# RWKV attention and a max-of-three feed-forward on one core: the order of 1593 pieces by one rank each instead of due times by kind and stage

## The chip, the cores and the metric

The kernel runs on 1 core of one Trainium2 chip. The metric is the device time of that core in microseconds (us); a smaller number is better. Five engines work beside each other, each through its own queue in order: TensorE (PE in the profile), VectorE (DVE), ScalarE (ACT), GpSimd (POOL), and SyncE (SP), which here only issues DMAs.

## What is computed

An attention with a decaying state, token by token, and a feed-forward network behind it. Shapes: batch 4, 8 heads, 768 tokens, head size 48; the feed-forward takes 3072 rows of 384 values through 768 hidden units.

```
for t in range(S):
    kt, vt, rt = (k[:, :, t], v[:, :, t], r[:, :, t])
    cur = np.einsum('bhd,bhe->bhde', u[None] * kt, vt)
    y[:, :, t] = np.einsum('bhd,bhde->bhe', rt, state + cur)
    state = w[None, :, :, None] * state + np.einsum('bhd,bhe->bhde', kt, vt)
...
h = np.maximum(np.maximum(x @ w1, x @ w2), x @ w3)
return (h @ w_out).astype(np.float32)
```

## The kernel before

**Tiling.** The 768 tokens are cut into 12 chunks of 64. A chunk's attention is done in two halves, q = 0 and q = 1, of 4 heads each. Per half PE makes the scores (`sc`), the values (`va`: scores times v, plus r times the state) and the update of the state (`ke`). A chunk's feed-forward is 18 groups `up` (6 blocks f of hidden units times 3 weight matrices i, each of 9 matmuls of 128x256, line 693) and the groups `dn` (three blocks of outputs, 18 matmuls each, mostly cut in two: 15 for f = 0 to 4 and 3 for f = 5). fp32 values are split into two fp16 numbers, a high and a low part; the high parts are made by ACT, the low parts by DVE (`kdl`, `ktdl`, `vdl`, `sdl`, `rl`, `al`: lines 449, 451, 490, 601) or POOL (`hl`, line 721). I write up c.f.i, dn c.m and sc, va, ke c.q, with the chunk first.

**Stages.** Chunks 0 and 1 take the attention's matmuls in fp32, chunks 2 and 3 in fp16 parts on 64-row corners of the array, and from chunk 4 on as 128-row matmuls of spread blocks, which SP copies with DMAs (`kb`, `ktb`, `vb`, `sb`, lines 436 and 437). In chunks 0 to 2 DVE scales k and r and makes the products; from chunk 3 on POOL does (lines 480, 499, 500, 516, 522). In the first 60 us the fp64 weights of the feed-forward are loaded as 8 "words" and made into fp16 parts (ACT lines 351 and 358, DVE lines 355 and 361); word 7 belongs to the second half of `dn`. 22 pieces `stir` of three matmuls each on zeros fill PE at the start.

**What an `up` holds.** Its result lies in one of four PSUM banks (`psm`). For i = 0 ACT copies it to a tile `m` (line 708), for i = 1 and 2 DVE takes the maximum into `m` (line 712), and only then is the bank free for the fourth next group. Then ACT makes `hh` of `m` (line 715) and POOL `hl`. `dn` takes a bank of the same four. `feat`, the tile of k and r by features, has two buffers; the load for the next chunk waits until the old one's last reader, the low part `rl`, is done.

**What sets the order.** The work is written as 1593 calls of `do`. Each gives an engine, a cost, what is read and written, which buffers are taken, and a due time of its own (`due`, in units of chunks). `Plan.order` is a list scheduler: of the pieces that can start earliest by its own clock, it takes the one with the smallest `due` and puts it behind the others on its engine. The result is the program's order on each engine, which the chip then follows. Before, a table `SHIFT` with one row for each kind of piece and one column for each of five stages was added to the due time. Costs are in `ISSUE`, `dma`, `helping` and the calls of `do`; `near` stands for DVE's low parts beside POOL.

**The end.** A check of the inputs' ranges ends in a flag (`count`, `flag`); every engine reads it once, ahead of the first piece in the program's order that touches dn 11.2 (line 1157), and a general path, not taken here, follows behind the program.

Of the kernel before, what the change touches and what calls it, by code (L numbers as in the profile page):

```python
# [7 lines left out]
F32 = mybir.dt.float32  # L8
# [10 lines left out]
P = 128  # L19
# [11 lines left out]
FEATURE = 2  # L31
HELPED = dict(scale=3, product=3, diagonal=3, decay=3)
# [41 lines left out]
class Plan:  # L74
# [6 lines left out]
    SHIFT = {  # L81
        "sp feat": (0.06, 2.41, 0.07, -2.37, 0),
        "sp tok": (4.64, -12.96, -5.22, 0.22, 0),
        "pe blank": (-0.35, 0, 0, 0, 0),
        "pool pad": (0, -0.41, -0.49, 0, 0),
        "dve kT": (0.95, 1.8, 0, 0, 0),
        "dve rT": (-2.97, 3.27, 0.98, 0, 0),
        "act ru": (-3.24, 2.09, 0, 0, 0),
        "pe bo": (-20.47, 6.44, 0, 0, 0),
        "dve am": (1.11, 102.24, -0.18, -0.19, 0.43),  # L90
        "pe sc": (-3.66, -0.77, -0.03, -0.83, -0.79),
        "pool vz": (-5.54, 0, 0, 0, 0),
        "act apart": (0.53, 0, 0, 0, 0),
        "pe va": (-1.26, 17.06, -22.44, -45.09, 3.03),
        "act xh": (-2.11, 6.29, 19.78, -2.05, -0.03),
        "dve xl": (-0.63, -5.4, -2.29, -1.83, 0.76),
        "act xsq": (0, -4.27, 17.76, -6.93, -1.42),
        "act u": (0, 1.78, 0, 0, 0),
        "dve tkf": (0, -7.35, 0, 0, 0),
        "pe turned": (0, -0.4, 0, 0, 0),  # L100
        "act tkt": (0, -2, 0, 0, 0),
        "pe stir": (0, 0.62, 1.56, 0.64, 1.31),
        "sp word": (3.62, 3.5, 0, 0, 0),
        "act ztop": (-5.52, -0.56, 0, 0, 0),
        "dve word": (2.04, 0, 0, 0, 0),
        "act his": (0.41, -4.8, 0, 0, 0),
        "dve lo": (1.13, -2.95, 0, 0, 0),
        "pe kp": (0.04, -16.13, 0, 0, 0),
        "act kt": (-0.4, -0.46, 0, 0, 0),
        "pe ke": (-10.27, -1.26, 0.08, 0, 0),  # L110
        "act state": (0, -0.83, 0, 0, 0),
        "act sq": (0, 0, -3.6, 6.45, -0.3),
        "act sd": (0, 14.27, 0, 0, 0),
        "dve state": (-1.48, -1.03, 1, -1.84, 0),
        "act sdh": (0, -0.64, 23.47, -0.59, 0),
        "dve sdl": (-4.22, 1.55, 7.23, -1.96, 0),
        "sp x3": (0, 2.95, -1.73, -0.89, 0.43),
        "pe up": (0, -3.62, 0.01, -0.2, -0.43),
        "act m": (-0.7, -4.9, 0, 1.38, -1.96),
        "dve m": (93.3, -556.17, 6.75, 0.9, 1.16),  # L120
        "act hh": (-2.49, -6.05, 2.12, -0.02, -11.37),
        "pool hl": (2.58, 5.89, 0.11, -4.17, 3.89),
        "dve hl": (0, -1.12, 1.62, 0, -0.03),
        "pe dn": (0, -1.32, -44.06, -0.15, 0.87),
        "act io": (0, -1.2, 1.65, -2.57, 0),
        "sp io": (0, -0.82, -6.31, -0.75, 2.37),
        "act kdh": (0, -1.05, -4.12, 0.03, 0.27),
        "dve kdl": (0, -5.77, 1.73, 1.56, 0),
        "act rh": (0, -2.11, 0, 2.07, 3.23),
        "dve rl": (0, 6.31, 0.65, 0.14, -1.72),  # L130
        "dve a": (0, -5.82, 10.67, 18.29, 0.93),
        "act am": (0, 0, 0.68, 0, 0),
        "act ah": (0, -2.27, 0, 24.09, -0.46),
        "dve al": (0, 1.56, -1.03, -0.22, -0.05),
        "dve kdec": (0, 3.63, -1, 0, 0),
        "act ktdh": (0, 8.15, -0.28, -1.81, 0),
        "dve ktdl": (0, -0.05, -0.41, -1.02, 0),
        "act vdh": (0, -0.74, 0, 2.92, -4.09),
        "dve vdl": (0, -1.06, 1.77, 0, 0.91),
        "pool kT": (0, 0, -8.52, 20.12, 0),  # L140
        "pool rT": (0, 0, -0.62, 12.91, -3.47),
        "pool am": (0, 0, 0, 0, 0.93),
        "pool kdec": (0, 0, -1.31, -0.98, 0),
        "sp sb": (0, 0, 0, 0.83, 0),
        "sp kb": (0, 0, 0, 33.45, 5.43),
        "sp ktb": (0, 0, 0, 0.5, 0),
        "sp vb": (0, 0, 0, 10.43, 3.71),
        "act wsq": (0, 0, 0, 1.63, 1.62),
        "sp again": (0, 0, 0, 0, 6.95),
        "dve ends": (0, 0, 0, 0, 3),  # L150
        "dve good": (0, 0, 0, 0, -2.56),
        "pe count": (0, 0, 0, 0, 1.34),
        "dve flag": (0, 0, 0, 0, 0.09),
    }
# [4 lines left out]
    def do(self, due, eng, cost, fn, reads=(), writes=(), takes=(), move=0, near=0, parts=1, counts=1.0, corner=False):  # L159


        n = len(self.todo)
        new = [t for _, t in takes]
        made = (*new, *writes, *reads)[0]
        kind = eng + " " + (made if isinstance(made, str) else made[0])
        stage = sum(due >= x for x in self.CLASSES)
        base = due
        due += self.SHIFT.get(kind, (0,) * 5)[stage]
        need = {self.wrote[k] for k in (*reads, *writes) if k in self.wrote}
        for k in writes:  # L170
# [85 lines left out]
def kernel(ctx, tc, feat, tok, wu, ut, ws, wo, cst, out):  # L256
# [29 lines left out]
    def load_tok(c, q):  # L286
        t = raw.tile([P, 3, 2, B, D], F32, name="tok")
        nc.sync.dma_start(out=t, in_=tok[c, q])
        raws.setdefault((c, q), {}).update(k=t[:, 0], r=t[:, 1], v=t[:, 2])
        return t  # L290

    def load_v(c, q):
        t = raw.tile([P, 2, B, D], F32, name="v1", bufs=4)
        nc.sync.dma_start(out=t, in_=tok[c, q][:, 2])
        raws.setdefault((c, q), {}).update(v=t)
# [307 lines left out]
    def keys(c, q):  # L603
        t = raws[c, q]
        t["ke"] = bank(D)
        if c < WHOLE:
            whole(t["ke"], D, (t.pop("kt") if c < FEATURE else units(t["k"]), units(t["v"])))
        else:
            split(c, t["ke"], [ktd[q]], [ktb], D, [lambda b, i: vd[q].dense[:, b, i, 0:D]])
# [261 lines left out]
    plan = Plan(dict(feat=2, tok=3, raw64=3, v1=4, ru=1, kt=1, psa=2, psv=2, psm=4, rh=2, rl=2, am=2, a=2, ah=2, al=2, x=2, m=3, io=3, hh=1, hl=1))  # L871
# [4 lines left out]
    def dma(due, fn, move, reads=(), writes=(), takes=(), eng="sp", n=1):  # L876
        do(due, eng, n * Plan.ISSUE[eng], fn, reads, writes, takes, move, 0, n)

    def helping(c, columns, what):
        return ("pool", 0.05 + 2.5e-3 * columns) if c >= HELPED[what] else ("dve", dve(columns))  # L880

# [147 lines left out]
    def leave_x(c, q, due):  # L1029
# [34 lines left out]
    def ffn(c):  # L1064
        x = [("xh", c), ("xl", c), ("x3", c)]
        for f in range(NF):
# [24 lines left out]
            do(due - 0.1, *(("dve", dve(TOK)) if lows_by(c, f) is nc.vector else ("pool", 0.7)), lo, reads=[m, ("hh", c, f), *([("hl", c)] if f else [])],  # L1091
# [76 lines left out]
def _layout(inputs):  # L1168
# [29 lines left out]
    tk = np.stack([tokm(inputs["k"]), tokm(inputs["r"]), tokm(inputs["v"])], axis=3)  # L1198
# [26 lines left out]
```

## Time and profile before

| | us |
|---|---|
| median of 3 runs | 382.52 (381.89 to 382.58) |
| the profiled execution | 382.55 |
| its span, first to last instruction | 380.8 |
| PE busy within the span | 373.0 |
| DVE, ACT, POOL busy | 250.3, 243.1, 188.8 |

The span is what the trace covers; 1.75 us of the execution lie outside it. A row of the trace has a start in us from the span's begin, then the time, engine, line and tiles, and in brackets the idle time of the engine ahead of it with what ended it. Matmuls overlap, so a group's own length is a little longer than its share of PE; the distance from one group's start to the next is what it costs.

### The profile page before, as it was taken

How to read it: one execution, taken by the hardware profiler on the slowest of the kernel's cores; microseconds unless marked ns; L12 is line 12 of the kernel's file. 1: busy time of each engine (PE TensorE's matmuls, PEld its weight loads, DVE VectorE, ACT ScalarE, POOL GpSimd, SP SyncE). 2: the span in 40 equal slices, each digit the busy share in tenths (PEclk: the TensorE clock that was granted, in tenths of full speed). 3: DMA queues.
4: the chain of work that ended last, by engine and by line, in shares of the span. 5: the costliest groups of instructions: out<-in, count | busy, mean ns of one | idle time of the engine just before them, and what ended most of it. 6: DMA issues, size and time to landing. Idle time of an engine off the chain costs nothing.

```text
span 380.8 us, 13578 instructions
## 1 busy us (share of the span) xinstructions
PE 373.0 (98%) x5660; PEld 335.8 (88%) x5660; DVE 250.3 (66%) x457; ACT 243.1 (64%) x623; POOL 188.8 (50%) x190
## 2 busy tenths in 40 slices
PE   8999999989999999999999999999999999999995
PEld 6888988878898999999899999999999999989885
DVE  5599999899968647558567667767567565123250
ACT  2899859788566647656556655755655935993621
POOL 8500333899995576466546647537836411020120
PEclk9999999999999999999999999999999999999999
DMA  8885836162995987969995996996996883740301
GB/s 293 324 305 188 339 123 216 72 241 59 286 271 129 257 243 198 273 157 289 271 262 144 268 274 173 265 262 185 247 246 190 213 205 89 245 137 17 99 2 49
DMA packets 28420, 77.12 MB, mean 203 GB/s; under 512 B 4865, under 2 KB 12993, under 8 KB 27329
## 3 DMA queue, kind: packets, MB, share of 16 engines
q1 hardware_dynamic: 28064, 75.96, 68.9%
q8 instruction: 46, 0.75, 0.8%
q10 hardware_dynamic: 288, 0.23, 0.2%
q14 instruction: 22, 0.17, 0.2%
HBM read 38.38 MB, written 4.72 MB: 113 GB/s over the span
## 4 chain that ended last, share of the span: by engine, by line
PE 84%; DVE 7%; issue 2%; DMA 2%; POOL 2%; ACT 1%; SPq 0%; POOLq 0%; DVEq 0%
PE psm L693 63%; PE psv L538 8%; PE psa L538 3%; PE psm L689 3%; PE psa L548 2%; PE psv L548 1%; DMA tok<-in_tok_dram 1%; PE psv L541 1%; DMA feat<-in_feat_dram 1%; PE psa L582 1%; DVE m L712 1%; POOL feat L480 1%; DVE kd L449 1%; DVE sd L451 1%; DVE vd L451 1%
## 5 line engine op out<-in xcount | busy, mean ns | idle before, releaser
L693 PEld LDWEIGHTS <-w 128*128 128x128 f16 x2592 | 249.2, 98 | 30.6 <-issue 1.8
L693 PE MATMUL psm<-x,w 128*128 128x256 f16 x1944 | 225.2, 273 | 1.0 <-DVE m L712 1.0
L721 POOL TENSOR_TENSOR hl<-m,hh 128x256 f16<-128x256 f32 x60 | 47.1, 786 | 125.0 <-ACT hh L715 125.0
L712 DVE SCALAR_TENSOR_TENSOR m<-psm,m 128x256 f32<-128x256 f32 x144 | 60.4, 419 | 59.5 <-PE psm L693 48.8
L715 ACT CAST hh<-m 128x256 f16<-128x256 f32 x72 | 28.9, 401 | 52.8 <-DVE m L712 52.5
L480 POOL TENSOR_TENSOR feat<-feat,wrt 128x512 f32<-128x512 f32 x36 | 51.2, 1440 | 20.5 <-DVE m L712 10.5
L693 PE MATMUL psm<-hh,w 128*128 128x256 f16 x432 | 55.8, 273 | 0.0
L463 ACT ACTIVATE junk<-tok 128x384 bf16<-128x384 f32 x72 | 37.3, 518 | 3.0 <-DMA tok<-in_tok_dram 2.0
L708 ACT ACTIVATE m<-psm 128x256 f32<-128x256 f32 x72 | 27.2, 378 | 16.8 <-PE psm L693 15.9
L693 PE MATMUL psm<-hl,w 128*128 128x256 f16 x216 | 33.4, 273 | 0.5 <-DVE hl L721 0.5
L499 POOL TENSOR_TENSOR am<-tok,u_sb 128x384 f32<-128x384 f32 x18 | 20.2, 1125 | 24.5 <-DVE al L601 20.4
L490 DVE TENSOR_TENSOR rl<-feat,rh 128x512 f16<-128x512 f32 x20 | 17.6, 880 | 11.4 <-ACT rh L485 11.4
L670 DVE SCALAR_TENSOR_TENSOR x<-psv,x 112x512 f16<-112x512 f32 (+2 forms) x24 | 16.1, 673 | 12.6 <-ACT x L667 12.6
L516 POOL TENSOR_TENSOR am<-cs,a 128x512 f32<-128x512 f32 x18 | 20.6, 1145 | 6.3 <-DVE a L507 6.1
L538 PE MATMUL psv<-rh,sb 128*128 128x64 f16 x256 | 23.6, 193 | 0.0
L538 PE MATMUL psv<-ah,vb 128*128 128x64 f16 x256 | 23.6, 193 | 0.0
L538 PE MATMUL psv<-al,vb 128*128 128x64 f16 x128 | 22.7, 193 | 0.0
L538 PE MATMUL psv<-rl,sb 128*128 128x64 f16 x128 | 22.7, 193 | 0.0
L538 PEld LDWEIGHTS <-vb 128*128 128x128 f16 x384 | 21.1, 98 | 0.4
L500 POOL TENSOR_TENSOR am<-am,tok 128x384 f32<-128x384 f32 x18 | 20.7, 1148 | 1.4
L738 ACT ACTIVATE io<-psm 128x256 f32<-128x256 f32 x36 | 13.0, 380 | 12.3 <-PE psm L693 12.0
L507 DVE TENSOR_REDUCE a<-am 128x8 f32<-128x384 f32 x20 | 11.0, 549 | 14.2 <-POOL am L500 14.2
(124 smaller groups left out, 580.1 us busy)
## 6 DMA issues: line engine op xcount, KB each, us to landing
tok<-in_tok_dram SPq DMA_DIRECT2D x26, 576.0 KB, 6.2
feat<-in_feat_dram SPq DMA_DIRECT2D x24, 512.0 KB, 4.8
raw<-in_ws_dram SPq DMA_DIRECT2D x6, 1152.0 KB, 7.7
kb<-kd SPq DMA_DIRECT2D x16, 256.0 KB, 5.6
vb<-vd SPq DMA_DIRECT2D x16, 256.0 KB, 5.9
sb<-sd SPq DMA_DIRECT2D x16, 256.0 KB, 5.5
out_dram<-io SPq DMA_DIRECT2D x31, 128.0 KB, 5.4
kb<-kd SPq DMA_DIRECT2D x16, 248.0 KB, 5.9
```

The source lines that it names most:

```text
L463: nc.scalar.activation(out=junk[:, 0:U * D].rearrange("p (u d) -> p u d", u=U), in_=src, func=AF.Square, scale=scale, accum_out=stat[:, ki ...
L480: helper(c, "scale").tensor_tensor(out=t[n], in0=t[n], in1=tb, op=ALU.mult)
L490: nc.vector.tensor_tensor(out=t["rl"], in0=units(t["rT"]), in1=t["rh"], op=ALU.subtract)
L499: helper(c, "product").tensor_tensor(out=w.rearrange("p (g b) d -> p g b d", g=2), in0=t["r"], in1=by_token(u_sb, q), op=ALU.mult)
L500: helper(c, "product").tensor_tensor(out=w, in0=w, in1=units(t["k"]), op=ALU.mult)
L516: helper(c, "diagonal").tensor_tensor(out=t["a"], in0=eye.unsqueeze(1).broadcast_to([P, U, C]), in1=t.pop("sum").unsqueeze(2).broadcast_to ...
L538: nc.tensor.matmul(out=ps[:, i, :], lhsT=block[k].on[a][i], rhs=prods[k](b, i), **flags)
L693: nc.tensor.matmul(out=ps, lhsT=a, rhs=b, start=first and n == 0, stop=last and n == len(prods) - 1)
L708: nc.scalar.mul(out=m, in_=ps, mul=by)
L712: nc.vector.scalar_tensor_tensor(out=m, in0=ps, scalar=by, in1=m, op0=ALU.mult, op1=ALU.max)
L715: nc.scalar.copy(out=h[0][:, f, :], in_=m)
L721: lows_by(c, f).tensor_tensor(out=h[1][:, f, :], in0=m, in1=h[0][:, f, :], op=ALU.subtract)
```

## The change

`SHIFT` goes, and with it the due times as an order. In its place stands `RANK`, a table with one number for each of the 1593 pieces, 0 to 1592, in the order in which they are written; `due` is set to it. The scheduler is otherwise the same: the rank decides only between pieces that can start at the same time by its clock, so a piece does not stand exactly where its rank says.

Several costs that the scheduler's clock uses are changed too: a DMA's issue is 0.58 for the spread copies and 0.74 for the copies inside x (0.45 before), POOL's work for the attention is 12% longer before chunk 6, and POOL's `hl` 0.82 before chunk 5 (0.7 before). No instruction's work changes by that. The three kinds of token tile stand as r, k, v in memory and not as k, r, v; sizes and numbers of loads stay. A new `FLIPPED` equals `FEATURE`, so that the new `load_kv` is never called.

```diff
+FLIPPED = 2
...
-    SHIFT = {
-        "sp feat": (0.06, 2.41, 0.07, -2.37, 0),
...
+    RANK = (
+        6, 51, 69, 17, 70, 33, 370, 317, 349, 309, 302, 280, 378, 412, 413, 410, 518, 331, 447, 700, 24, 39, 20, 13,
...
-        due += self.SHIFT.get(kind, (0,) * 5)[stage]
+        due = self.RANK[n]
...
-        raws.setdefault((c, q), {}).update(k=t[:, 0], r=t[:, 1], v=t[:, 2])
+        raws.setdefault((c, q), {}).update(r=t[:, 0], k=t[:, 1], v=t[:, 2])
...
-    def dma(due, fn, move, reads=(), writes=(), takes=(), eng="sp", n=1):
-        do(due, eng, n * Plan.ISSUE[eng], fn, reads, writes, takes, move, 0, n)
+    def dma(due, fn, move, reads=(), writes=(), takes=(), eng="sp", n=1, each=0.45):
+        do(due, eng, n * each, fn, reads, writes, takes, move, 0, n)
...
-        return ("pool", 0.05 + 2.5e-3 * columns) if c >= HELPED[what] else ("dve", dve(columns))
+        return ("pool", (1.12 if c < 6 else 1.0) * (0.05 + 2.5e-3 * columns)) if c >= HELPED[what] else ("dve", dve(columns))
...
-            dma(due, lambda: spread(nc.sync, dst, src), 2.4, reads=[*keys, *(("pad", n) for n in range(14))], writes=[name], n=2)
+            dma(due, lambda: spread(nc.sync, dst, src), 2.4, reads=[*keys, *(("pad", n) for n in range(14))], writes=[name], n=2, each=0.58)
...
-            do(due - 0.1, *(("dve", dve(TOK)) if lows_by(c, f) is nc.vector else ("pool", 0.7)), lo, reads=[m, ("hh", c, f), *([("hl", c)] if f else [])],
+            do(due - 0.1, *(("dve", dve(TOK)) if lows_by(c, f) is nc.vector else ("pool", 0.82 if c < 5 else 0.7)), lo, reads=[m, ("hh", c, f), *([("hl", c)] if f else [])],
...
-    tk = np.stack([tokm(inputs["k"]), tokm(inputs["r"]), tokm(inputs["v"])], axis=3)
+    tk = np.stack([tokm(inputs["r"]), tokm(inputs["k"]), tokm(inputs["v"])], axis=3)
```

In the rows below, lines of the change stand one lower than those of before (L360 for L361, and so on).

**DVE, around the end of the weights' conversion.** `w7` is the low part of word 7 (line 361), `raw64` its upper step (line 355), `feat` a scaling of k or r of chunk 2 in place (line 480), `rl` the low part of r that frees a `feat` buffer, `m` the maxima of the feed-forward. Before:

```order
L355 SCALAR_TENSOR_TENSOR raw64_773<-raw64_773,ztop1_113 128x1152
L712 SCALAR_TENSOR_TENSOR m_923<-psm_899,m_923 128x256
L480 TENSOR_TENSOR feat_795<-feat_795,wrt_127 128x512
L712 SCALAR_TENSOR_TENSOR m_923<-psm_911,m_923 128x256
L480 TENSOR_TENSOR feat_795<-feat_795,wrt_127 128x512
L361 SCALAR_TENSOR_TENSOR w7_110<-raw64_773,w7_110 128x1152
L449 TENSOR_TENSOR kd0_140<-feat_795,kd0_140 128x8x64
L712 SCALAR_TENSOR_TENSOR m_972<-psm_978,m_972 128x256
L670 SCALAR_TENSOR_TENSOR x_802<-psv1_159,x_802 112x512
L712 SCALAR_TENSOR_TENSOR m_972<-psm_996,m_972 128x256
L451 SCALAR_TENSOR_TENSOR vd0_144<-tok_800,vd0_144 128x8x48
L490 TENSOR_TENSOR rl_1035<-feat_795,rh_991 128x512
```

Of the change:

```order
L489 TENSOR_TENSOR rl_968<-feat_793,rh_954 128x512
L711 SCALAR_TENSOR_TENSOR m_703<-psm_926,m_703 128x256
L711 SCALAR_TENSOR_TENSOR m_937<-psm_956,m_937 128x256
L498 TENSOR_TENSOR am_1032<-tok_808,u_sb_101 128x384
L499 TENSOR_TENSOR am_1032<-am_1032,tok_808 128x384
L354 SCALAR_TENSOR_TENSOR raw64_789<-raw64_789,ztop1_113 128x1152
L711 SCALAR_TENSOR_TENSOR m_1051<-psm_1039,m_1051 128x256
L506 TENSOR_REDUCE a_1067<-am_1032 128x8
L479 TENSOR_TENSOR feat_871<-feat_871,wrt_127 128x512
L711 SCALAR_TENSOR_TENSOR m_1051<-psm_1053,m_1051 128x256
L360 SCALAR_TENSOR_TENSOR w7_110<-raw64_789,w7_110 128x1152
L479 TENSOR_TENSOR feat_871<-feat_871,wrt_127 128x512
```

`rl` of chunk 2, behind `w7` before, now stands ahead of it, and chunk 2's products and the scaling of its second half have come in between.

**ACT, the same place.** `psm_1070` is the result of up 1.1.0, `kd1` the high part of chunk 2's scaled k, which reads the last row above. Before, `kd1` and the first `m` of chunk 1:

```order
L738 ACTIVATE io_1089<-psm_1037 128x256
L485 CAST rh_1091<-feat_989 128x512
L514 ACTIVATE am_1054<-cs_99,a_1087 128x64 x8
L444 ACTIVATE kd1_141<-feat_989 128x8x64
L738 ACTIVATE io_1173<-psm_1068 128x256
L444 ACTIVATE ktd1_143<-tok_993 128x8x48
L708 ACTIVATE m_1191<-psm_1161 128x256
```

Of the change:

```order
L513 ACTIVATE am_1032<-cs_99,a_1067 128x64 x8
L707 ACTIVATE m_1113<-psm_1091 128x256
L714 CAST hh_761<-m_1051 128x256
L443 ACTIVATE kd1_141<-feat_871 128x8x64
L707 ACTIVATE m_1136<-psm_1070 128x256
```

On PE three groups of chunk 1 (up 1.1.0, 1.0.0, 1.0.1) now run ahead of dn 0.1 and dn 0.0, which came first; dn 0.0 takes the bank that `m_1136<-psm_1070` frees, and that copy stands behind `kd1`.

**DVE, in chunk 2's feed-forward.** `psm_2577` is up 2.4.1, `psm_2472` up 2.1.2 (before: `psm_2586` and `psm_2411`). Before:

```order
L712 SCALAR_TENSOR_TENSOR m_2375<-psm_2411,m_2375 128x256
L601 TENSOR_TENSOR al_2439<-am_2020,ah_2425 128x512
L449 TENSOR_TENSOR kd0_140<-feat_2256,kd0_140 128x8x64
L712 SCALAR_TENSOR_TENSOR m_2455<-psm_2441,m_2455 128x256
L712 SCALAR_TENSOR_TENSOR m_2455<-psm_2460,m_2455 128x256
L507 TENSOR_REDUCE a_2485<-am_2457 128x8
L490 TENSOR_TENSOR rl_2565<-feat_2256,rh_2552 128x512
L712 SCALAR_TENSOR_TENSOR m_2539<-psm_2541,m_2539 128x256
L712 SCALAR_TENSOR_TENSOR m_2539<-psm_2555,m_2539 128x256
L712 SCALAR_TENSOR_TENSOR m_2604<-psm_2586,m_2604 128x256
```

Of the change:

```order
L711 SCALAR_TENSOR_TENSOR m_2400<-psm_2472,m_2400 128x256
L450 SCALAR_TENSOR_TENSOR sd1_147<-state_154,sd1_147 128x8x48
L448 TENSOR_TENSOR kd0_140<-feat_2207,kd0_140 128x8x64
L448 TENSOR_TENSOR ktd0_142<-tok_1541,ktd0_142 128x8x48
L489 TENSOR_TENSOR rl_2589<-feat_2207,rh_2572 128x512
L448 TENSOR_TENSOR ktd1_143<-tok_1729,ktd1_143 128x8x48
L711 SCALAR_TENSOR_TENSOR m_2587<-psm_2577,m_2587 128x256
```

Five low parts, of five tiles, now stand between two maxima where three stood among four other maxima.

More of the change, by code (lines that the diff above doesn't have):

```diff
@@ L80 @@
     CLASSES = (0.0, 1.0, 2.0, 10.0)
-    SHIFT = {
-        "sp feat": (0.06, 2.41, 0.07, -2.37, 0),
[L83 to L154, printed above, removed]
@@ L156, in __init__ @@
+    RANK = (
[67 rows of a table added]
+    )
     def __init__(self, bufs):
@@ L288, in load_tok, with load_kv @@
         nc.sync.dma_start(out=t, in_=tok[c, q])
-        raws.setdefault((c, q), {}).update(k=t[:, 0], r=t[:, 1], v=t[:, 2])
+        raws.setdefault((c, q), {}).update(r=t[:, 0], k=t[:, 1], v=t[:, 2])
         return t
+    def load_kv(c, q):
+        t = raw.tile([P, 3, 2, B, D], F32, name="tok")
+        nc.sync.dma_start(out=t[:, 1:], in_=tok[c, q][:, 1:])
+        raws.setdefault((c, q), {}).update(k=t[:, 1], v=t[:, 2])
     def load_v(c, q):
-        t = raw.tile([P, 2, B, D], F32, name="v1", bufs=4)
+        t = raw.tile([P, 2, B, D], F32, name="v1", bufs=2 * FLIPPED)
         nc.sync.dma_start(out=t, in_=tok[c, q][:, 2])
@@ L606, in keys @@
         if c < WHOLE:
-            whole(t["ke"], D, (t.pop("kt") if c < FEATURE else units(t["k"]), units(t["v"])))
+            whole(t["ke"], D, (t.pop("kt") if c < FLIPPED else units(t["k"]), units(t["v"])))
         else:
@@ L868, in general @@
                     put(m, leaving(ps, P, 1.0))
-    plan = Plan(dict(feat=2, tok=3, raw64=3, v1=4, ru=1, kt=1, psa=2, psv=2, psm=4, rh=2, rl=2, am=2, a=2, ah=2, al=2, x=2, m=3, io=3, hh=1, hl=1))
+    plan = Plan(dict(feat=2, tok=3, raw64=3, v1=2 * FLIPPED, ru=1, kt=1, psa=2, psv=2, psm=4, rh=2, rl=2, am=2, a=2, ah=2, al=2, x=2, m=3, io=3, hh=1, hl=1))
     do = plan.do
@@ L904, in fetched @@
         dma(due, lambda: load_feat(c, q), 1.8, reads=behind, writes=["fetched"], takes=[("feat", ("feat", c, q))])
+        if c < FLIPPED:
+            dma(due, lambda: load_v(c, q), 0.85, reads=behind, writes=["fetched"], takes=[("v1", ("tok", c, q))])
+            return
         if c < FEATURE:
-            dma(due, lambda: load_v(c, q), 0.85, reads=behind, writes=["fetched"], takes=[("v1", ("tok", c, q))])
+            dma(due, lambda: load_kv(c, q), 1.67, reads=behind, writes=["fetched"], takes=[("tok", ("tok", c, q))])
             return
@@ L912, in late_squares @@
         dma(due, lambda: do_tile(t, load_tok(c, q)), 2.5, reads=[("begun", int(due))], writes=["fetched"], takes=[("tok", t)])
-        for kind, n in enumerate((1, 0, 2)):
+        for kind, n in enumerate(range(3)):
             do(due + 0.2, "act", 0.62, lambda kind=kind, n=n: square_sum(units(T[t][:, n]), kind, c, q), reads=[t], writes=[("sq", c, q, "rkv"[kind])])
@@ L959, in before_keys @@
         t = ("tok", c, q)
-        if c < FEATURE:
+        if c < FLIPPED:
             do(due - 0.30, "pe", 0.94, lambda: flipped(c, q), reads=[("feat", c, q), ("kT", c, q)], takes=[("psa", ("kp", c, q))], counts=0.5, corner=True)
@@ L1042, in leave_x @@
             if c:
-                dma(due + 0.06, lambda: x_last(T["x", c]), 0.4, reads=[hi, lo], writes=[rest], n=2 * NJ)
+                dma(due + 0.06, lambda: x_last(T["x", c]), 0.4, reads=[hi, lo], writes=[rest], n=2 * NJ, each=0.74)
             do(due + 0.9, "act", 0.97, lambda: x_sum(c, T["x", c]), reads=[hi, rest], writes=[("xsq", c)])
```

66 rows, old and new, of the table RANK are left out of this document.

## The prediction

> **What bounds the kernel now.** First the page's busy times, then a table of windows: for each stretch its length, then the busy time of PE, of PE's weight loads, DVE, ACT and POOL (with instructions in brackets), the granted clock, and the DMA engines' share and rate. Last, what PE waited for.
>
> ```profile
> span 380.8 us, 13578 instructions
> ...
> PE 373.0 (98%) x5660; PEld 335.8 (88%) x5660; DVE 250.3 (66%) x457; ACT 243.1 (64%) x623; POOL 188.8 (50%) x190
> ...
> 0.00:25.00 25.00, 23.36 (x459) 19.61 (x460) 15.83 (x30) 16.02 (x31) 13.47 (x24) 1.00 0.85 310
> 25.00:60.00 35.00, 35.00 (x617) 31.35 (x615) 34.23 (x52) 28.04 (x53) 7.09 (x5) 1.00 0.58 208
> 60.00:100.00 40.00, 38.19 (x926) 33.49 (x921) 37.04 (x58) 31.67 (x91) 33.80 (x28) 1.00 0.53 173
> 100.00:160.00 60.00, 60.00 (x842) 54.62 (x840) 40.10 (x75) 36.48 (x100) 41.39 (x39) 1.00 0.86 231
> 160.00:260.00 100.00, 99.54 (x1411) 91.00 (x1409) 67.64 (x119) 58.74 (x154) 58.04 (x58) 1.00 0.87 237
> 260.00:376.90 116.90, 116.86 (x1427) 105.69 (x1425) 55.46 (x127) 71.79 (x198) 35.01 (x38) 1.00 0.56 149
> 376.90:380.80 3.90, 0.00 (x0) 0.00 (x0) 0.00 (x0) 0.38 (x1) 0.00 (x0) 1.00 0.16 50
> ...
> PE psv L682 <- DVE still L277: 1.1, 1, 1.1
> PE psm L693 <- DVE m L712: 1.0, 1, 1.0
> PE psv L541 <- DVE x L670: 0.7, 1, 0.7
> PE psa L548 <- issue: 0.6, 1, 0.6
> PE psm L693 <- DVE hl L721: 0.5, 1, 0.5
> ```
>
> PE is the bound from 1.1 to 376.9 us, and the change gives it the same matmuls. So the new time is the old one, less the waits that go, plus the waits and turns that come. Of PE's 7.8 idle us, 1.1 lie ahead of its first matmul and 3.9 behind its last (copy out and landing, which the new order has as well). What an order can win is the rest: 0.58 in the first 25 us, 1.81 between 60 and 100, 0.46 at dn 4, **2.85 us in all, 0.7%**. The clock is 1.00 in every stretch, so nothing is to be had there. The other reading of the table matters as much: from 25 to 100 us DVE is busy 71.3 of 75 us. In that stretch there are two full engines, and a new order on DVE is paid there.
>
> **Waits that go.** The 1.81 us of chunks 1 to 3 are PE waiting for DVE's `x` and `m`. Since DVE is nearly full there, they go only if PE comes later or DVE's low parts come quicker. The first happens (below), so I take 1.3 of the 1.81 away and leave 0.5, the bounds being 0 and 1.81. The 0.46 at dn 4.0 is the wait for the last `hl`; between the last `up` of chunk 4 and its use the new order has one more group, up 5.0.0 (0.98 us), so all of it goes. The 0.58 at 14 us waits for nothing that the trace shows; I leave it, with 0 and 1.2 as ends. Together **-1.8**.
>
> **Turns.** Each passage of PE between 64-row corners and the whole array costs:
>
> ```profile
> 17.06 0.72 PE psv L548 x32
> ...
> 25.07 0.98 PE psm L693 x9
> 26.05 0.85 PE psv L548 x32
> ...
> 28.77 1.09 PE psm L693 x9
> ```
>
> In this chain of waits the same `ke` takes 0.72 behind another corner group and 0.85 behind an `up`; an `up` takes 0.98 behind whole-array work and 1.09 behind corners. That is 0.12 a turn. PE's order has 38 turns before and 42 now, all before 120 us: **+0.5**.
>
> **First new wait: dn 0.0.** First, DVE and POOL hold each other up:
>
> ```profile
> 49.20 0.41 DVE L712 SCALAR_TENSOR_TENSOR m<-psm,m 128x256 f32<-128x256 f32 x1
> 49.53 0.83 DVE L480 TENSOR_TENSOR feat<-feat,wrt 128x512 f32<-128x512 f32 x1
> 50.61 0.68 DVE L480 TENSOR_TENSOR feat<-feat,wrt 128x512 f32<-128x512 f32 x1
> 51.21 1.35 DVE L361 SCALAR_TENSOR_TENSOR w<-raw,w 128x1152 f16<-128x1152 f32 x1
> 52.48 1.16 DVE L449 TENSOR_TENSOR kd<-feat,kd 128x512 f16<-128x512 f32 x1
> ...
> 57.88 0.55 DVE L507 TENSOR_REDUCE a<-am 128x8 f32<-128x384 f32 x1
> ...
> 51.23 1.86 POOL L721 TENSOR_TENSOR hl<-m,hh 128x256 f16<-128x256 f32 x1 [1.42 <-ACT hh L715]
> 63.61 2.71 POOL L480 TENSOR_TENSOR feat<-feat,wrt 128x512 f32<-128x512 f32 x2 [10.53 <-DVE m L712]
> ...
> 367.08 0.67 POOL L721 TENSOR_TENSOR hl<-m,hh 128x256 f16<-128x256 f32 x1 [3.53 <-ACT hh L715]
> ```
>
> `hl` takes 0.67 alone and 1.86 when `w7` (line 361) has begun just before it; the `kd` behind that waits for `hl` and takes 1.16 in place of 0.68; a scaling begun while `hl` runs takes 0.83 in place of 0.68. Whoever is second waits for nearly the rest of the first. The rows do not show a weight step (line 355 or 361) that finds POOL at work already. [...]
>
> Now the race, from the end of up 0.5.1, with these rows and:
>
> ```profile
> 50.48 0.38 ACT L708 ACTIVATE m<-psm 128x256 f32<-128x256 f32 x1
> ...
> 51.04 0.64 ACT L444 ACTIVATE kd<-feat 128x512 f16<-128x512 f32 x1
> 51.57 0.62 ACT L485 CAST rh<-feat 128x512 f16<-128x512 f32 x1
> ...
> 53.25 1.26 PE L693 MATMUL psm<-hh,w 128*128 128x256 f16 x10
> ...
> 54.89 1.25 PE L693 MATMUL psm<-hh,w 128*128 128x256 f16 x10
> ...
> 59.19 4.26 DMA feat<-in_feat_dram
> ```
>
> PE has up 0.5.2, three groups of chunk 1 and dn 0.1 ahead of dn 0.0: 4 x 0.98 + 1.64 (53.25 to 54.89) = 5.56 us. Then it needs the bank of up 1.1.0. That bank waits for ACT, ACT's copy for `kd1`, and `kd1` for DVE's row of six: maximum 0.33 (49.20 to 49.53), sum 0.47, scaling 0.60, maximum 0.33, `w7` 1.27 (51.21 to 52.48), scaling 0.69, together 3.69; ACT 0.53 for `kd1` (51.04 to 51.57) and 0.38; about 0.25 for the three hand-overs: 4.85. Undisturbed, PE has 0.7 to spare.
>
> But POOL comes in. `rl`, which frees the `feat` buffer for chunk 3, now stands ahead of the last two weight steps. The load takes 4.26 us; DVE's work from there to `w7` is about 4.7 (three maxima, two products of 0.5, a weight step of 1.3, sum, scaling, maximum). So POOL's two scalings of chunk 3 (2.71, some 1.27 each undisturbed) start about 0.4 ahead of `w7`. Before, they ran at 63.6, past all this. `w7` is held 0.75 and the scaling behind it 1.1. That makes 6.7 against 5.56: a wait of 1.15. If DVE is also late by 0.5, as a queue that is 98% full tends to be, 1.65; if the load lands a microsecond later, `w7` comes first, 0.75 goes, and 0.4 remains; if nothing collides, 0. I take **+1.2**.
>
> **Second new wait: up 2.5.0**, which needs the bank that `m_2587<-psm_2577` frees. Chain and timeline:
>
> ```profile
> 74.69 0.80 DVE rl L490
> 75.49 1.27 DVE vd L451
> 76.76 1.27 DVE sd L451
> ...
> 78.37 0.94 DVE ktd L449
> ...
> 107.93 1.40 PE psv L538 x48
> ```
>
> From the end of up 2.1.2 PE has six `up` and one `va` to do: 6 x 0.98 + 1.40 = 7.28. DVE has a maximum, five low parts, a maximum. Alone the five would take 2.6 (0.68 for two of 512, 0.55 for three of 384, less 0.08 of overlap each). In the rows above, with POOL at work, four take 4.28, which makes 5.35 for five, and 6.35 at the 1.27 of the longest. With the maxima and hand-overs that is 3.6, 6.3 or 7.3 against 7.28, and a low part stands ahead of the first maximum as well, up to 0.9 more. So 0 to 0.9. POOL is busy 85% and 69% in the two stretches around, so the disturbed rows are the nearer: **+0.5**.
>
> **Sum.** 382.55 (the profiled execution, 0.03 over the median of 382.52) - 1.8 + 0.5 + 1.2 + 0.5 = 382.95, **383.0**: a gain on old waits that is spent on turns and two new ones.
>
> **Rivals.**
> - *Slower: DVE and POOL collide everywhere.* Both new waits at their full price, 1.65 and 0.9, and the 1.81 of chunks 1 to 3 stays: 382.55 - 0.46 + 0.5 + 1.65 + 0.9 = 385.1. It decides by whether POOL's scaling of chunk 3 begins ahead of `w7` and DVE is then late by half a microsecond. For it speaks DVE's 71.3 of 75 us; against it, that each new wait makes PE late and gives DVE time for the next one. 0.18.
> - *Faster: no collision forms.* All 2.27 go, only the turns come: 380.8, and 380.2 if the 0.58 goes as well. Chunk 3's `feat` would have to land over 2 us later than I reckon; or DVE has a reserve that I do not see. 0.25.
> - *A spread copy loses its cover.* `kb` for sc 6.0 can start only when sc 5.1 is done; in PE's order 7.5 us of work stand between them now, 10.4 before.
>
> ```profile
> kb<-kd SPq DMA_DIRECT2D x16, 256.0 KB, 5.6
> ...
> kb<-kd SPq DMA_DIRECT2D x16, 248.0 KB, 5.9
> ```
>
> Two issues, about 1.2, and 5.9 to landing make 7.1, which just fits; a landing 2 us above the median costs 1.5 on top of the forecast: 384.5. 0.08.
> - *The order matters nowhere*, since PE is full: 382.5. 0.05.
>
> **Chances.** The forecast has 0.44, its own range 382.2 to 383.8. Under about 0.2% (0.76 us) a measurement of this kernel cannot be told from no change. Faster by more: the second rival and a little of the forecast, 0.27. Within: the last rival and three quarters of the forecast, 0.38. Slower by more: the first and third rivals and the forecast's upper end, 0.35. The range that leaves out no more than 2 in 10 reaches from the second rival to just short of the first: 380.7 to 384.9.
>
> **What would show it.** PE waits: `x` and `m` of chunks 1 to 3 mostly gone, `hl` at dn 4 gone; a wait of about 1 us near 60 us for ACT's `m`, behind a DVE scaling longer than 1 us and a POOL scaling that starts before 58; another near 114 for DVE's `m` behind five low parts. DVE's busy time would be longer between 25 and 60, its low parts above 1 us there. The forecast is wrong if PE shows no wait between 50 and 65 us (then faster), or waits of more than 3 us between 50 and 120 (then slower), or a wait for `kb` or `ktb`, for which I have taken nothing.

## The result, and the profile after

| | before | the change |
|---|---|---|
| median | 382.55 us (4 runs, 381.89 to 383.58) | 385.91 us (4 runs, 385.51 to 386.87) |
| ratio to before | | 1.0093, 95% interval 1.0069 to 1.0116 |
| profiled execution, its span | 382.55, 380.8 | 385.51, 383.7 |

The change makes the kernel 0.9% slower, by 3.4 us; the forecast was 383.0 with 384.9 as its upper end. PE's last matmul ends 2.7 us later than before. The page's busy times of the change:

```profile
PE 373.5 (97%) x5660; PEld 335.3 (87%) x5660; DVE 253.1 (66%) x457; ACT 242.4 (63%) x623; POOL 191.6 (50%) x190
```

Its table of windows, cut as before:

```profile
0.00:25.00 25.00, 22.99 (x464) 18.97 (x466) 16.59 (x29) 16.57 (x32) 13.47 (x24) 1.00 0.88 327
25.00:60.00 35.00, 34.38 (x603) 30.25 (x600) 32.40 (x45) 26.94 (x48) 9.46 (x8) 1.00 0.61 228
60.00:100.00 40.00, 37.01 (x824) 32.44 (x822) 35.34 (x59) 30.07 (x84) 24.82 (x22) 1.00 0.39 122
100.00:160.00 60.00, 59.51 (x917) 53.95 (x915) 46.91 (x80) 37.93 (x102) 47.28 (x42) 1.00 0.83 227
```

And what PE waited for (us in total, times, the longest):

```profile
PE psv L540 <- issue: 2.5, 2, 1.7
PE psv L681 <- DVE still L271: 1.1, 1, 1.1
PE psa L581 <- issue: 0.9, 1, 0.9
PE psm L692 <- DVE w L360: 0.6, 1, 0.6
PE psm L692 <- DVE m L711: 0.5, 1, 0.5
PE psm L692 <- DVE hl L720: 0.4, 1, 0.4
```

Of the waits that before had, DVE's `x` and `m` (0.67 and 1.01) and `hl` at dn 4 (0.46) are gone. Three waits for DVE are new, 1.55 together, about as forecast. What was not forecast is the first row: PE stands 2.5 us more for "issue", that is, for nothing that this view knows. These are the places in PE's timeline:

```profile
14.27 0.43 PE L581 MATMUL psa<-dg,feat 64*64 64x48 f32 x8 [0.95 <-issue]
...
59.31 0.50 PE L692 MATMUL psm<-hh,w 128*128 128x256 f16 x3 [0.62 <-DVE w L360]
62.65 0.27 PE L692 MATMUL psm<-hl,w 128*128 128x256 f16 x1 [0.44 <-DVE hl L720]
68.45 0.21 PE L540 MATMUL psv<-rh,sd 64*48 64x64 f16 x1 [0.85 <-issue]
81.97 0.45 PE L540 MATMUL psv<-vd,ktd 64*48 64x48 f16 x22 [1.66 <-issue]
116.28 1.91 PE L692 MATMUL psm<-x,w 128*128 128x256 f16 x16 [0.49 <-DVE m L711]
```

The three "issue" pauses stand in the middle of a piece, between two matmuls of the same kind, and the trace names nothing that they wait for. What is common to them shows when PE's records (weight loads, matmuls, and some 85 others) are counted from 0 in the order of their starts: the instruction behind each pause is number 449, 2497 and 3009. All three are 193 modulo 256, and so is the one behind the pause of before, 449:

```profile
14.65 0.56 PE L548 MATMUL psa<-feat 64*64 64x64 f32 x12 [0.58 <-issue]
```

The page of the change tells what comes in such blocks:

```profile
q8 instruction: 46, 0.75, 0.8%
```

This DMA queue, which the page calls "instruction", carries 46 packets of 16 KB (0.75 MB) during the execution, about one for every 248 of PE's 11,407 instructions. I take them for PE's own code, which the times below and e1 and e2 bear out. The trace has the start and the length of each packet. Worked out from these, for some blocks (us):

```
kernel  block starts   PE enters      its code is     PE enters   PE stood
        at number      the one before  fetched         it          there
before      449           9.61        12.28 - 13.36    14.65       0.80
before     2497          64.39        65.39 - 66.33    69.53       0
before     2753          69.53        70.20 - 71.63    74.80       0
before     3009          74.80        74.25 - 75.66    79.74       0
change      449           8.99        11.77 - 12.80    14.27       1.16
change     2497          65.33        66.09 - 67.24    68.45       1.04
change     2753          68.45        69.56 - 70.59    76.40       0
change     3009          76.40        79.52 - 80.44    81.97       1.83
```

(The last column is the distance between two starts, and a little more than the idle time in the rows above.) The fetch of a block begins about when PE enters the block ahead of it: in all twelve profiles told of here, 518 such fetches, it began from 1.8 us ahead of that border to 4.9 us behind it (median 1.2). It took 0.88 to 1.80 us (median 1.07), and PE never entered the block less than 1.21 us after its fetch had ended; where it stood, it mostly went on 1.2 to 1.6 us behind. Of the 43 pauses in these profiles 42 stand at a border; the other, 0.19 us, is in e7. So in these runs a block has to last about 3 us (from border to going on, 3.12 at 2497 in the table), and 5 to 6 where the next one's fetch starts late (5.57 at 3009). Behind `up` groups it does: 18 instructions in 0.98 us make 14 us a block. A block of corner pieces doesn't: sc 2.1 and va 2.0, which the change puts next to each other, use up 256 instructions in 2.09 us.

### The profile page after: what moved, and what is told of

It reads as the page before. It is cut to its first block, busy times and chain, and to the rows that moved or that the text cites. A ratio compares the mean times of both kernels' runs of the same rounds, so it can differ in the third digit from the quotient of the medians.

```text
span 383.7 us, 13553 instructions
## 1 busy us (share of the span) xinstructions
PE 373.5 (97%) x5660; PEld 335.3 (87%) x5660; DVE 253.1 (66%) x457; ACT 242.4 (63%) x623; POOL 191.6 (50%) x190
## 4 chain that ended last, share of the span: by engine, by line
PE 86%; DVE 8%; issue 2%; POOL 2%; ACT 1%; ACTq 0%
PE psm L692 65%; PE psv L537 8%; PE psa L537 3%; PE psm L688 3%; PE psa L547 2%; PE psv L547 2%; PE psv L540 1%; PE psa L581 1%; DVE m L711 1%; DVE feat L479 1%; POOL feat L479 1%; DVE ktd L448 1%; PE psa L540 1%; DVE kd L448 1%; DVE sd L450 1%
## 5 line engine op out<-in xcount | busy, mean ns | idle before, releaser
L720 POOL TENSOR_TENSOR hl<-m,hh 128x256 f16<-128x256 f32 x60 | 45.6, 765 | 142.1 <-ACT hh L714 141.7
L692 PE MATMUL psm<-hh,w 128*128 128x256 f16 x432 | 56.7, 273 | 0.6 <-DVE w L360 0.6
L479 POOL TENSOR_TENSOR feat<-feat,wrt 128x512 f32<-128x512 f32 x36 | 50.0, 1400 | 5.3 <-DMA feat<-in_feat_dram 4.2
L498 POOL TENSOR_TENSOR am<-tok,u_sb 128x384 f32<-128x384 f32 x18 | 23.3, 1295 | 18.7 <-DVE al L600 12.1
L515 POOL TENSOR_TENSOR am<-cs,a 128x512 f32<-128x512 f32 x18 | 22.0, 1223 | 6.7 <-DVE a L506 6.6
L590 DVE COPY_PREDICATED am<-cs,psa 128x512 f32<-128x512 int32 x24 | 17.6, 735 | 10.8 <-PE psa L537 5.3
L489 DVE TENSOR_TENSOR rl<-feat,rh 128x512 f16<-128x512 f32 x20 | 16.3, 817 | 9.5 <-ACT rh L484 9.5
L521 POOL TENSOR_TENSOR tok<-tok,tkt 128x384 f32<-128x384 f32 x16 | 19.6, 1226 | 5.9 <-ACT junk L462 5.8
L499 POOL TENSOR_TENSOR am<-am,tok 128x384 f32<-128x384 f32 x18 | 19.9, 1107 | 1.4
```

The costliest lines, as they stand in the source:

```text
L479: helper(c, "scale").tensor_tensor(out=t[n], in0=t[n], in1=tb, op=ALU.mult)
L498: helper(c, "product").tensor_tensor(out=w.rearrange("p (g b) d -> p g b d", g=2), in0=t["r"], in1=by_token(u_sb, q), op=ALU.mult)
L499: helper(c, "product").tensor_tensor(out=w, in0=w, in1=units(t["k"]), op=ALU.mult)
L515: helper(c, "diagonal").tensor_tensor(out=t["a"], in0=eye.unsqueeze(1).broadcast_to([P, U, C]), in1=t.pop("sum").unsqueeze(2).broadcast_to ...
L521: helper(c, "decay").tensor_tensor(out=t["k"], in0=t["k"], in1=by_token(tkt, q), op=ALU.mult)
L692: nc.tensor.matmul(out=ps, lhsT=a, rhs=b, start=first and n == 0, stop=last and n == len(prods) - 1)
```

## The experiments

Each is one of the two kernels with one edit; the order on the other engines stays unless it is named. "Change" is 385.91 us above, before is shared by the runs of one group (medians 382.97 for e1 to e4, 382.07 for e5 to e7, 383.02 for e8 and e9, 382.52 for e10). "Pauses" is PE's idle time put down to "issue" in the profiled execution. For e2 that is its longest, 393.90 us; the median of its other five is 390.57, and four of them have mean clocks of 0.990 to 0.996.

| run | median, us | ratio to before | pauses, us |
|---|---|---|---|
| e1, change, code moved by 48 | 385.52 | 1.0064 (1.0041 to 1.0087) | 4.6 |
| e2, change, code moved by 112 | 391.46 | 1.0206 (1.0162 to 1.0250) | 8.3 |
| e3, before, code moved by 112 | 385.12 | 1.0058 (1.0035 to 1.0080) | 2.3 |
| e4, change, POOL swapped | 389.52 | 1.0163 (1.0123 to 1.0202) | 3.1 |
| e5, change, corner pieces apart | 384.79 | 1.0068 (1.0041 to 1.0095) | 3.6 |
| e6, change, copies ahead | 388.80 | 1.0195 (1.0148 to 1.0242) | 5.0 |
| e7, change, maximum first | 386.26 | 1.0105 (1.0074 to 1.0135) | 5.1 |
| e8, e5 and two moves | 385.95 | 1.0103 (1.0068 to 1.0139) | 1.6 |
| e9, change again | 387.59 | 1.0135 (1.0098 to 1.0171) | 4.1 |
| e10, e8 mended | 385.73 | 1.0084 (1.0060 to 1.0108) | 2.8 |

**e1 and e2: the same order, the code moved.** Filler matmuls on zeros are cut into narrower ones, so that everything behind them stands 48 or 112 places further on in PE's code.

```diff
         for _ in range(3):
-            nc.tensor.matmul(out=T["stir"], lhsT=still[:, 0:P], rhs=still, start=True, stop=True)
+            k = T["stirs"] = T.get("stirs", -1) + 1
+            parts = 4 if 40 <= k < 48 else 1
+            w = TOK // parts
+            for j in range(parts):
+                nc.tensor.matmul(out=T["stir"][:, j * w:(j + 1) * w], lhsT=still[:, 0:P], rhs=still[:, j * w:(j + 1) * w], start=True, stop=True)
```

> The change with eight filler matmuls of 256 columns (16 to 25 us) cut into four of 64 each: the same columns, 48 more instructions on PE, so that all of PE's code behind them lies 48 places further on; nothing else moves. Theory 'code': PE stood at 68.45 and 81.97 us because the next block of 256 of its instructions had not arrived. Then both stalls go (nothing over 0.3 us that waits for 'issue' behind 60 us), the one at 14 us stays at about 0.9, and the time is 385.9 - 0.85 - 1.66 + 0.1 = 383.5, up to 384.6 if DVE is late next. Rival 'place': these matmuls wait for something of their own (a turn of the array, a semaphore the trace does not show). Then both stalls stay in the same pieces and the time is 385.9 to 386.1.

> The same with 112 more instructions instead of 48. Theory 'code': the block borders now fall so that one block is used up by ke 2.0 and va 2.1 alone (about 1.8 us) and a later one by scores and state update of chunks 3 and 2 near 86 us. The stalls at 68.4 us and inside ke 3.0 go, and new ones stand in va 2.1 near 77 us (1.2 to 3.4 us, as the loads of chunk 4 are under way then) and near 86 to 88 us (about 1), each with PE's instruction count at 193 modulo 256; 385.6 to 388.0. Rival 'place': the old stalls stay where they were, nothing new; 386.0.

Both moved the pauses. Behind 60 us, neither e1 nor e2 stands at a matmul where the change stood; every pause of both is at 193 modulo 256 again, and so at other matmuls (e1: 449, 705, 961, 3009, 4289). PE's timeline of e2, where the two largest are:

```profile
92.60 0.20 PE L540 MATMUL psv<-vd,ktd 64*48 64x48 f16 x2 [4.04 <-issue]
...
114.12 2.12 PE L696 MATMUL psm<-x,w 128*128 128x256 f16 x18 [2.13 <-issue]
```

Ahead of the first of them a block lasted 1.88 us, while its successor's fetch began 3.66 us after it was entered. This settles where the pauses come from, and rules out "place". The times were missed all the same. For e1 I expected 383.5, 2 less than came: two pauses went, and others came in the first 26 us, at 83 us (0.52) and at 112 us (1.06), most of them at borders that had just been in time before. For e2 I expected 388.0 at most. The pause foreseen near 77 us didn't come, since the code was fetched from 76.20, ahead of the border at 77.37; the one foreseen near 88 us came there, but of 4.04 us and not of about 1, with 3.41 us at half the clock behind it (from 92.82); and the one of 2.13 was not foreseen.

**e3: the order of before, its code moved.** The edit of e2, in the kernel before.

> The kernel before with the same 112 more instructions. Theory 'code': the order of before can be made to stand too: its corner pieces of chunk 2 near 69 to 71 us now fill a block that lasts 1.8 us, and a stall of about 1.2 us appears there that was not there before; the waits for DVE's x and m at 75 and 78 us (1.7) become shorter by as much, so the time rises by only 0.2 to 1.0, to 382.7 to 383.5 (more if the early stall grows too). Rival 'place': no new stall, 382.5 to 382.8.

```profile
72.37 0.48 PE L541 MATMUL psv<-vd,ktd 64*48 64x48 f16 x24 [0.96 <-issue]
```

The pause is where it was expected, at number 2753, behind a block that lasted 1.84 us. The time rose by 0.6% with no piece moved at all, more than expected: the early pause grew from 0.58 to 1.0, and one of 0.3 came at 88 us. How the code lies can cost before two thirds of what the new order costs.

**e4: the first new wait, from its cause.**

```diff
     order = plan.order(dict(pe=1.1, dve=5.1, act=5.0, pool=5.2, sp=1.2))
+    for n, m in ((341, 347), (342, 341)):
+        p = plan.todo[n]
+        order.remove(p)
+        order.insert(order.index(plan.todo[m]) + 1, p)
```

341 and 342 are POOL's scalings for chunk 3, 347 its first product `am`; n is put right behind m.

> The change with POOL's first product for chunk 3 (am) moved ahead of the two scalings of chunk 3, so that POOL does not begin on them ahead of w7. Theory 'collision': w7 falls from 2.08 to about 1.35 us, PE's two waits at 59 and 62.6 us (1.06 together) fall to 0.4 or less, and the time falls by 0.5 to 1.0 if nothing behind takes it up, to 384.9 to 385.4; the code stalls stay. Rival 'full queue': DVE is late by its own work, w7 stays near 2 us or another operation is held in its place, the waits stay at 0.8 to 1.1, 385.9.

In the change POOL's scalings begin at 55.08 and `w7` behind them takes 2.08; here POOL stands idle beside `w7`. Two rows of DVE's timeline of the change, then one of POOL's:

```profile
57.17 2.08 DVE L360 SCALAR_TENSOR_TENSOR w<-raw,w 128x1152 f16<-128x1152 f32 x1
59.17 1.48 DVE L479 TENSOR_TENSOR feat<-feat,wrt 128x512 f32<-128x512 f32 x1
```

```profile
55.08 2.96 POOL L479 TENSOR_TENSOR feat<-feat,wrt 128x512 f32<-128x512 f32 x2 [1.07 <-PE psm L692]
```

The same two views of e4:

```profile
57.42 1.34 DVE L360 SCALAR_TENSOR_TENSOR w<-raw,w 128x1152 f16<-128x1152 f32 x1
63.55 1.74 DVE L448 TENSOR_TENSOR kd<-feat,kd 128x512 f16<-128x512 f32 x1 [0.52 <-POOL feat L479]
```

```profile
61.80 2.95 POOL L479 TENSOR_TENSOR feat<-feat,wrt 128x512 f32<-128x512 f32 x2 [0.30 <-ACT kd L443]
```

What PE waits for in e4, and then four windows of it:

```profile
PE psv L540 <- issue: 2.2, 1, 2.2
PE psa L540 <- DVE rl L489: 1.4, 1, 1.4
...
PE psv L540 <- DVE al L600: 0.5, 1, 0.5
```

```profile
64.00:68.00 4.00, 1.88 (x68) 1.34 (x68) 4.00 (x5) 2.52 (x9) 2.13 (x2) 1.00 0.29 40
68.00:71.40 3.40, 3.40 (x98) 3.02 (x93) 3.37 (x7) 2.05 (x5) 2.11 (x2) 0.50 0.56 194
82.00:85.00 3.00, 0.82 (x49) 0.72 (x48) 2.55 (x4) 2.06 (x7) 2.13 (x2) 1.00 0.81 256
85.00:88.50 3.50, 3.50 (x27) 2.47 (x20) 1.16 (x3) 0.89 (x3) 0.67 (x1) 0.51 0.84 296
```

The collision is gone and so are its two waits, 1.06; but POOL's scalings now meet the low parts of chunk 2, and PE waits 1.4 for `rl` and 0.5 for `al`. And something came that neither theory had: after PE had been idle for about 2.1 of the 4 us up to 68, and for 2.2 before 84.67, the granted clock is 0.5 for 3.41 us (the clock's records: 68.03 to 71.44, 85.09 to 88.50). That is 1.7 us each. The time rose instead of falling.

**e5: the corner pieces apart.** Groups of `up` go between them, one and two: (n, m) are va 2.0 behind up 1.0.2, and ke 3.0 with its state's update behind up 1.4.0 and up 1.5.0.

```diff
+    for n, m in ((242, 282), (365, 318), (366, 365)):
```

> The change with two corner pieces taken away from their neighbours on PE: up 1.0.2 moved between sc 2.1 and va 2.0, and up 1.4.0 and up 1.5.0 moved ahead of ke 3.0. Theory 'code': the block of 256 instructions that began at 65.3 us lasts 3.1 us in place of 2.1, the one that began at 76.4 lasts about 5.4 in place of 3.7, so the stall of 1.04 shrinks to 0.3 or less and the one of 1.83 goes; two turns more cost 0.24. 385.9 - 2.5 + 0.24 = 383.6, up to 384.8 if a later block meets a busy DMA queue. Rival 'conserved': PE being early only makes another block or DVE late, the sum of PE's waits between 60 and 120 us stays within 0.7 of the change's, 385.2 to 386.2.

Both pauses went, as expected. Others came, which PE's waits show:

```profile
PE psa L540 <- issue: 1.4, 1, 1.4
PE psa L547 <- issue: 1.3, 1, 1.3
...
PE psa L581 <- issue: 1.0, 1, 1.0
```

The block entered at 82.58 lasted 3.78 us and the next one's code was fetched only from 85.73, with the loads of chunk 4 and the copies of x under way; in this execution the border 961 stood too, at 25 us. 384.79 is just within the expected range, whose end is 384.8. But the pauses are 3.6 us together here and 3.5 in the change, and the intervals of the two ratios overlap, so that the time does not show a gain.

**e6: data ahead of the code.**

```diff
+        if p["n"] == 339:
+            spare = dram.tile([2, P, 2 * U * P], F16, name="spare")
+            for k in range(2):
+                nc.sync.dma_start(out=spare[k], in_=kd[0].flat)
         p["fn"]()
```

> The change with two more DMAs on SP ahead of the load of feat for chunk 3, second half: each copies kd0 (512 KB) to a place in DRAM that nobody reads; they can start when kd0 is written, at about 64.4 us. Theory 'code behind data': PE's code is fetched by the same 16 DMA engines, so the fetch that began at 66.1 us begins 1.5 to 4 us later, and the stall near 68 us grows from 1.04 to 2.5 to 5 us, with the clock halved for 3.4 us behind it if it exceeds 2; 387.5 to 392. Rival 'code has a way of its own': the fetch still begins 0.8 us after the block border, the stall stays at 0.8 to 1.3; only feat comes later by 2 to 5 us, and the time rises by 0 to 1.5.

The code of block 2497 was fetched from 67.13, 1.67 us behind the border in place of 0.77, and PE stood 1.78 there in place of 1.04:

```profile
69.34 0.21 PE L540 MATMUL psv<-rh,sd 64*48 64x64 f16 x1 [1.59 <-issue]
83.17 0.45 PE L540 MATMUL psv<-vd,ktd 64*48 64x48 f16 x22 [1.97 <-issue]
```

So the code came 0.9 us later behind copies of 1 MB, less than the 1.5 to 4 that I expected. At this border the seven profiles of the change and its variants that have neither copies nor moved code show 0.68 to 1.41; this run alone is weak evidence that code waits for data, and the medians over all profiles, further down, are the better one. The pause at 83 us, a little longer than the change's, is followed by 3.41 us at half the clock, which the change's own is not. 388.80 is within the expected range, but mostly by this, about 1.7 us, and not by the pause at 68 us that I had in mind.

**e7: the second new wait, from its cause.** The maximum of up 2.4.1 goes ahead of the last low part.

```diff
+    for n, m in ((438, 603),):
```

> The change with the maximum of up 2.4.1 moved ahead of the last of the five low parts on DVE. Theory 'low parts': PE's wait of 0.49 near 116 us goes, nothing comes for it, and the time falls by 0.2 to 0.5, to 385.4 to 385.7. Rival 'full queue': the low part comes later by as much and va or ke of chunk 4 waits for its spread copy instead; 385.9.

The wait at 116 us went. The time didn't fall: this execution had pauses of 5.1 us, and 1.3 for a copy at 233 us. A term of 0.5 can't be told by the time where the pauses differ by more between executions.

**e8, e9, e10: further apart, and the change again.** e8 adds to e5 that ke 2.1 stands behind up 1.5.2, and e7's move. In e8 ke 2.1 multiplies the high part of chunk 3's v, so that e8 computes something else; e10 moves ACT's `vdh` behind it as well (chunk 3's by the kernel's numbers; the text for e10 says chunk 4).

```diff
+    for n, m in ((242, 282), (365, 318), (366, 365), (273, 322), (274, 273), (390, 274), (438, 603)):
```

> The kernel of e5 with two moves more: ke 2.1 behind up 1.5.1 and up 1.5.2, and the maximum of up 2.4.1 ahead of the last low part (as in e7). Theory 'code': the block that began at 82.6 us in e5 lasts 5.8 us in place of 3.8, its stall of 1.56 goes; of PE's stalls at block borders those behind 60 us are 0.5 or less together, the early ones stay. 384.8 - 1.5 - 0.3 = 383.0 (382.4 to 384.2): no slower than before by more than 0.4%. Rival 'conserved': another block or DVE is late instead, 384.4 to 386.

> The change itself once more, to see what of its stalls is the same in another execution. Theory 'code': stalls stand at the same places of PE's code (193 modulo 256: the borders 449, 2497 and 3009), with lengths that differ by up to 1 us as the DMA queue differs, and perhaps at 961; 385.5 to 386.9. Rival 'accident': the places differ from the first profile's, most of them gone or elsewhere than at a border.

> The kernel of e8, with ACT's vdh of chunk 4 (second half) also moved behind ke 2.1, which had read it in place of chunk 2's. Theory 'code': as e8's profile, the stalls at block borders behind 60 us are 0.7 or less together (the change: 2.9, and 2.8 in e9) and the early one or two (14 us, 25 us) stay; about as far below the change as e5 or further: 383.0 to 385.0, with the clock's mean at 0.998 to 1.0 in all executions. Rival 'conserved': 385 to 387, with other waits of DVE or DMA in place of the stalls.

e8 had no pause above 0.5 us behind 60 us, as expected, but its median of 385.95 is far over 382.4 to 384.2. e9 is the same program as the change, in another execution:

```profile
PE psv L540 <- issue: 2.0, 2, 1.1
PE psa L547 <- issue: 1.3, 1, 1.3
...
PE psv L537 <- DMA vb<-vd: 1.0, 1, 1.0
...
PE psa L581 <- issue: 0.7, 1, 0.7
```

Its pauses stand at 449, 961, 2497, 3009 and 3265: the first profile's three, and two more that had just been in time. Its median is 1.7 us above the change's first; the mean clock of four of its six executions is 0.994 to 0.996, where one stretch at half the clock makes 0.9956 (3.41 x 0.5 / 387), while in the 48 executions of before that were beside these experiments it was never under 0.998. e10 has short pauses at five borders, and is no faster than e5 (385.73 and 384.79, ratios to before whose intervals overlap): the expected 383 to 385 was missed. Its pauses behind 60 us are 1.8 us together and not 0.7, the longest of 0.85 behind the block of sc 3.1 and sc 3.0, which still lasted 3.8 us; and one of its six executions has a mean clock of 0.993. So single moves take a pause away at one border, and the next border takes part of it back. None of these versions beats before.

## Why the prediction was wrong

Its terms, against the profiled execution (PE's idle time and busy time):

| term | forecast | measured |
|---|---|---|
| waits for `x`, `m` and `hl` that go | -1.8 | -2.27 (2.14, and 0.13 for `rl` that stood in the 1.81) |
| four turns more | +0.5 | +0.5 at most (PE busy 373.0 to 373.5, which also holds the start behind one stop more) |
| first new wait, near 60 us | +1.2 | +1.06 |
| second new wait, near 116 us | +0.5 | +0.49 |
| PE's code at block borders | 0 | +2.88 (0.58 to 3.46) |
| sum | +0.4 | +2.7, as PE's last matmul: 376.9 to 379.6 |

**What held.** PE is the bound, and every term that the forecast had was right in sign and nearly in size. The mechanism of the first wait was right, its place not quite: POOL's scalings began at 55.08, before `w7`, which took 2.08 (forecast 1.27 + 0.75), the scaling behind it 1.48 (forecast 1.8); but PE stood for `w7` itself and for the `hl` behind it, in the `dn` groups, not for the bank of up 1.1.0. That two waits with other causes add up to nearly the forecast 1.2 is in part luck. For the 0.75 that `w7` is held in the forecast, no row of before has a case: it was my estimate, from pairs in which `hl`, a `kd` or a scaling came second. The runs showed `w7` at 2.08 beside POOL's scaling (the change) and at 1.34 without it (e4), 0.74 apart. The second wait came as drawn, behind low parts that take 1.16 to 1.40 each beside POOL's work, where before has `rl` at 0.68 (55.28) and `vd` at 0.54 (54.82) with POOL idle. DVE's timeline of the change:

```profile
110.86 1.40 DVE L448 TENSOR_TENSOR kd<-feat,kd 128x512 f16<-128x512 f32 x1 [0.28 <-ACT kd L443]
112.19 1.35 DVE L448 TENSOR_TENSOR ktd<-tok,ktd 128x384 f16<-128x384 f32 x1
113.46 1.16 DVE L489 TENSOR_TENSOR rl<-feat,rh 128x512 f16<-128x512 f32 x1
114.54 1.35 DVE L448 TENSOR_TENSOR ktd<-tok,ktd 128x384 f16<-128x384 f32 x1
115.81 1.20 DVE L711 SCALAR_TENSOR_TENSOR m<-psm,m 128x256 f32<-128x256 f32 x3
```

`kb` and `ktb` were in time in the profiled execution. DVE's busy time from 25 to 60 us did not grow (34.23 to 32.40): fewer instructions fell into that stretch.

**What failed** is the step "The 0.58 at 14 us waits for nothing that the trace shows; I leave it". That pause was the only trace in the profile of before of the thing that decides: a border of PE's code. By leaving it as a constant, the sum had no term for what the new order does to code. The step on turns had the same hole from the other side: it priced the passage into and out of the corners, and not a row of corner pieces in itself. PE's order of before keeps `up` groups between them, so that no block behind 15 us was used up before the next had come; the shortest, 3.49 us, met an idle queue (no data packet under way at its start, 90.08). In the change a block of 2.09 us and one of 3.74 us stand where 3.1 and 5.6 us pass from border to going on. So PE's waits between 50 and 120 us are 4.1 us together, over the 3 that the prediction had named as a sign that it is wrong, and 2.5 of them are code.

The late fetch behind the border at 76.40 us fits what was in the DMA queue. SP's timeline of the change:

```profile
74.78 0.34 SPq L282 DMA_DIRECT2D tok<-in_tok_dram  x1
75.22 0.37 SPq L277 DMA_DIRECT2D feat<-in_feat_dram  x1
76.37 0.33 SPq L282 DMA_DIRECT2D tok<-in_tok_dram  x1
```

These loads, 576, 512 and 576 KB, were asked for just ahead of the border, and the fetch began 3.1 us behind it. No run takes these loads away; but over all profiles the fetch begins a median of 0.36 us behind the border where at most two data packets are under way at the border, and 1.58 where twelve or more are, and e6 points the same way. A border cost PE nothing where the block ahead of it outlasted its successor's fetch: the one that the change enters at 68.45 us lasted 7.95 us, the next one's code was there after 2.14 of them (70.59), and PE stood 0.

**The rivals.** The time came out near the slower one (385.1), but not by its mechanism: PE stood for a collision of DVE and POOL near the two places that were forecast and nowhere else, and the old waits did go. e4 shows why that is no reserve: the collision taken away at 57 us came back at 62 us.

**What stays open** is what the new order would be worth if code always came in time. By the other rows of the table it would stand 0.2 us under before, but no run shows that: every edit that took a pause away brought another. e3 shows that the time of before hangs on where its code lies as well.

## What to carry to other kernels

Look at pauses of an engine that the profile puts down to nothing: count its instructions up to each, and see whether they fall on a grid. Where many short instructions stood in a row here, the code itself was a transfer with a rate: where PE stood, 256 instructions per about 3 us at best (3.12 at 2497 of the change), and mostly per 5 to 6 (5.04 at 449 of before, 5.28 and 5.57 at 449 and 3009 of the change). A planner that gathers such pieces to save turns needs that as a cost. Orders that differ by less than a few us should be compared over several executions, with the pauses of each.

## What the runs showed of the hardware

- PE's code arrived in 46 DMA packets of 16 KB, one block ahead, and its fetch began later where data was under way: 0.36 us behind the border as a median with at most two data packets under way, 1.58 with twelve or more, 4.9 at most.
- PE's clock halved for 3.41 us after idle times of 2.0 to 2.2 us in one stretch or spread over 3 (e4, e6) and of 4.04 (e2), and not after one of 1.66 (the change), nor after 2.13 in e2 (the pause before 114.12). Inside the run the lengths of the clock's records are multiples of 3.41 us (in e4 3.41, 13.65, 3.41 and 300.37; in the change 378.88, 111 times as long). Cut into steps of that length, and worked out from the idle times of all twelve profiles, each step in which PE was idle for 1.97 us or more was followed by half the clock, no step with 1.59 or less was, and the 2.13 of e2 lie across two steps, 1.31 in the first.
- One program's pause at a border differs by up to 1.3 us between executions: at 961 none in the change and 1.28 us in e9.
